# The order of the elements in the tile of exp(L): pairs of heads outermost or innermost

## The chip, the core and the metric

The kernel runs on one core of one Trainium2 chip. The metric is the device time of one execution in microseconds (us); lower is better. TensorE is called PE in the profile (its weight loads PEld), VectorE DVE, ScalarE ACT, GpSimd POOL, and SyncE, which issues most of the transfers, SP.

## What is computed

The reference is a gated recurrence over time, one state of 48 x 48 for each of 4 batches and 8 heads, and then a normalised two-layer perceptron with a residual:

```python
state = np.zeros((B, H, D, D), dtype=np.float32)          # B, H, S, D = 4, 8, 768, 48
for t in range(S):
    state = alpha[:, :, t, :, None] * state + np.einsum('bhd,bhe->bhde', k[:, :, t], v[:, :, t])
    y[:, :, t] = np.einsum('bhd,bhde->bhe', q[:, :, t], state)
x = y.transpose(0, 2, 1, 3).reshape(B, S, H * D)          # B, S, 384
xn = (x - mu) / np.sqrt(var + 1e-06) * g_ln
out = x + np.maximum(xn @ w_ch1, 0.0) @ w_ch2              # 384 -> 1536 -> 384
```

## The kernel before

Time is cut into 6 chunks of 128 steps. A chunk of one batch is one run of the generator `attention(c, b)`, so there are 24 of them; the kernel names them a, b, c, ... x in this order (a to d are chunk 0 for the four batches, e to h chunk 1, and so on). Within a chunk the recurrence becomes matrix products: with L the running sum of log(alpha), q is multiplied by exp(L) and k by exp(-L), and the state that goes into the next chunk is multiplied by a **gate**, which is exp(L) at the last step. Chunk 0 is treated as one piece of 128 steps, so it has one gate; each later chunk is treated as two halves of 64 steps and has two gates.

The partitions of a tile hold the 128 steps, and a row holds 8 heads x 48 channels. The heads are taken in pairs: a pair's two heads stand 64 apart, padded from 48 to 64, so that a transposed pair fills 112 partitions (R = 64 + 48). The steps of `attention` that matter here, with their lines:

- L289: log of alpha on ScalarE; L294 or L471: the running sums L on TensorE, into PSUM.
- L299: ScalarE writes exp(L) into the tile `eq`; L300: it writes exp(-L) back into PSUM. For the runs whose `eq` lies in a shared buffer, the profile calls that tile `more`.
- L302 and L304: VectorE multiplies k by exp(-L) and q by exp(L) into `qk`.
- L309: SP stores the rows of `eq` that hold the gates (one row in chunk 0, two after it) into a small buffer `row` in device memory, 2 KB a row.
- L320: TensorE transposes the pairs of `qk`; L325 and L327 copy the results out of PSUM (`kT`, `qT`). L337 and L487 are the scores, L346 and L351 mask them on VectorE.
- L357: SP fetches the gates from `row` as columns, one value for each of the 112 partitions and each of the 4 pairs, into the tile `gate`.
- L367: TensorE makes the update of the state. In chunk 0, L376 multiplies it by the gate on VectorE; in later chunks L380 adds on VectorE and L382 multiplies by the gate on GpSimd.
- L392 or L408: the output products; L417 to L460: the normalisation and a transpose into `xT`; L430 keeps x in device memory.

The weights arrive in twelve pieces as 64-bit numbers (L207). VectorE and ScalarE turn each into float32 (L219 to L229; VectorE reads and writes every second 32-bit word there). Three buffers hold the raw pieces, so a later piece is loaded only when an earlier one is decoded. The perceptron of chunk 0 is plain products (L514, L526); for later chunks the two layers are computed with fewer block products, whose operands VectorE prepares by sums (L586, L613, L752, L777), and whose results VectorE, ScalarE and GpSimd combine (L803 to L854 and L626 to L705).

All of these are generators. A string of letters and digits, `ORDER`, says which generator goes one step on next, and each engine runs its own instructions in that order. SP's queue is in that order too: a load that waits there holds back the loads behind it.

At the end of the kernel the tiles `eq` serve once more as plain buffers for sums of `xT` (L554 to L556), seen as flat rows.

Of the kernel before, what the change touches and what calls it, by code (L numbers as in the profile page):

```python
# [9 lines left out]
FP32 = mybir.dt.float32  # L10
# [38 lines left out]
def kernel(  # L49
# [36 lines left out]
    nc = tc.nc  # L86

    B, S, H, D = q.shape
    DM = H * D
    DF = w_ch1.shape[1]  # L90
    P = 128
    NCB = S // P
    NP = H // 2
    R = 64 + D
# [5 lines left out]
    cpool = ctx.enter_context(tc.tile_pool(name="const", bufs=1))  # L100
# [144 lines left out]
    for _ in range(8):  # L245
# [4 lines left out]


    shared = more.rearrange("p i m -> p (i m)")[:, :4 * NP * P]
    eqs = [cpool.tile([P, NP, 2, 64], FP32, name=f"eq{b}") for b in range(2)]
    eqs += [shared[:, i * NP * P:(i + 1) * NP * P].rearrange(
        "p (a b c) -> p a b c", b=2, c=64) for i in range(2)]
    qks = [cpool.tile([P, 2, NP, 2, 64], FP32, name=f"qk{b}") for b in range(3)]
    qks.append(shared[:, 2 * NP * P:].rearrange("p (i a b c) -> p i a b c", i=2, b=2, c=64))
    sts = [[cpool.tile([R, NP, D], FP32, name=f"st{b}_{i}") for i in range(2)] for b in range(B)]
    for b in range(B):
        nc.vector.memset(eqs[b].rearrange("p a b c -> p (a b) c")[:, :, D:], 0.0)  # L260
        nc.vector.memset(qks[b].rearrange("p i a b c -> p (i a b) c")[:, :, D:], 0.0)


# [1 line left out]
    def eq_of(c, b):  # L265
        return eqs[b if c < 2 else b % 2]

    def qk_of(c, b):
        return qks[b if c < 2 else b % 3]
# [10 lines left out]
    def attention(c, b):  # L280
# [3 lines left out]
        odd = 0 if whole else b % 2  # L284

        qk = qk_of(c, b).rearrange("t n p i c -> t n i p c")[:, :, :, :, :D]
        eq = eq_of(c, b).rearrange("t p i c -> t i p c")[:, :, :, :D]
        la = work.tile([P, 2, NP, D], FP32, name="la", tag="row", bufs=8)
        nc.scalar.activation(out=la, in_=raws.pop(("a", c, b)), func=AFT.Ln)  # L289
        las[c, b] = la.rearrange("t i p d -> t (i p d)")  # L290
# [14 lines left out]
        ends = slice(P - 1, P) if whole else slice(HS - 1, P, HS)  # L305
        ne = 1 if whole else 2
        row = dram.tile([2, 2 * 64 * NP], FP32, name="row", tag="row")
        gate = work.tile([P, 2, NP], FP32, name="gate", tag="gate", bufs=B)
        nc.sync.dma_start(row[:ne], eq_of(c, b)[ends].rearrange("o p i c -> o (p i c)"))  # L309
        yield  # L310
        at = ats[b % len(ats)]
        if not whole:
# [41 lines left out]
                mask=mask_of_halves.unsqueeze(1).broadcast_to([P, 2 * NP, HS]))  # L354
        yield
        with nc.allow_non_contiguous_dma(reason="two rows to columns"):
            nc.sync.dma_start(gate[:R, :ne], row[:ne].rearrange("o (p r) -> r o p", p=NP)[:R])  # L357
        yield
        vn = raws["v", c, b]
        heads = [slice(0, 64), slice(64, R)]  # L360
# [28 lines left out]
        for p in range(NP):  # L389
# [4 lines left out]
            for n in range(0 if whole else 8):  # L394

                if odd:
                    inner, s, i = n // 4, n // 2 % 2, n % 2
                    r = i
                else:
                    i, s, r = n // 4, n // 2 % 2, n % 2  # L400
# [144 lines left out]
    def buffers_of_last():  # L545

        more_x = work.tile([P, NF, B, P], FP32, name="xT", tag="xT").rearrange("p f b t -> p (f b t)")
        free = [raw.tile([P, 2, 2, NP, D], FP32, name=f"r{n}", tag="in", bufs=6).rearrange(
            "t b i p d -> t (b i p d)") for n in "akq"]
        h = [t.rearrange("k p i s t -> k (p i s t)") for t in ats]  # L550
        h += [t.rearrange("t n p i c -> t (n p i c)") for t in qks[:3]]
        h.append(more_x[:, :NT * HB * P])
        late_of["h"] = [t.rearrange("p (j b t) -> p j b t", b=HB, t=P) for t in h]
        sums = [t.rearrange("t p i c -> t (p i c)") for t in eqs[:2]]  # L554
        sums += [more_x[:, NT * HB * P:]] + [t[:, 512:] for t in free]
        late_of["x"] = [t[:, i * HB * P:(i + 1) * HB * P]  # L556
                        for t in sums for i in range(t.shape[1] // (HB * P))]
        late_of["u"] = [t[:, :512] for t in free]
# [198 lines left out]
    def combine_x(c):  # L757
        b = x_blocks(c)
        new = []
        if c + 1 == NCB:  # L760
            buffers_of_last()
            new = late_of["x"]
        for i in range(0 if new else 5):
            t = work.tile([P, NT, P], FP32, name=f"sum{i}", tag="sum", bufs=11)
            t = t.rearrange("p a t -> p (a t)")
            new += [t[:, k * HB * P:(k + 1) * HB * P] for k in range(2)]
        t101, t103, t100, m7, t102, m10, m9, m13, m8 = new[:9]
        add, sub = nc.vector.tensor_add, nc.vector.tensor_sub
        ready = x_ready(c)
        for n, op, out, x, y in (  # L770
                (None, sub, t101, b[1], b[3]), (2, sub, t100, b[4], b[5]),
                (1, add, t103, b[2], t100), (7, add, m7, t101, t103),
                (14, sub, t102, b[0], t100), (10, sub, m10, t102, t101),
                (3, sub, t101, t101, b[5]), (9, sub, m9, b[0], b[4]),
                (5, add, b[4], b[2], b[4]), (13, sub, m13, t103, b[3]),
                (8, sub, m8, t102, b[1])):
            op(out, x, y)  # L777
            if n is not None:
                ready[n] = out
            yield  # L780
# [99 lines left out]
    turns |= {"PQ"[h]: second_of_chunk_0(h) for h in range(2)}  # L880
    turns |= {"4": sums(), "5": scores()}
    turns |= {chr(ord("a") + n): attention(n // B, n % B) for n in range(NCB * B)}
    turns |= {chr(ord("A") + i): take_weights(i) for i in range(len(pieces))}
    turns |= {"M": mlp(), "V": hidden_products(NCB - 1), "S": combine_first(), "W": combine_weights(), "R": relus(),
# [34 lines left out]
```

## Time and profile before

| what | us |
|---|---|
| time, median of 3 runs | 432.96 (431.92 to 435.25) |
| the profiled execution's own time | 433.59 |
| its span in the profile | 431.5 |
| TensorE busy | 421.3 |
| VectorE busy | 331.7 |
| ScalarE busy | 205.8 |
| GpSimd busy | 151.8 |

The span is the time from the first to the last instruction of the program; busy time is the sum of an engine's instructions without overlap. The profile also has 52,797 packets of transfers, 45.36 MB in all. An instruction's line in a view reads: start, duration, engine, line of the kernel, operation, what it writes and reads, and in brackets how long its engine stood idle before it and what ended that. A group's line has the total busy time, the mean duration in ns, and the idle time before its members.

### The profile page before, as it was taken

What the parts mean: (1) busy time and instruction counts of PE and PEld (TensorE: products, weight loads), DVE (VectorE), ACT (ScalarE), POOL (GpSimd) and SP (SyncE); (2) the same over time, 40 slices, a digit from 0 to 9 for tenths busy, and PEclk for the clock granted to TensorE, in tenths of its full rate; (3) what the DMA queues carried; (4) which work ended last, traced back from release to release, by engine and by line L of the source; (5) the groups of instructions that cost most, each with busy time, mean ns of one, the idle gap of its engine ahead of it and who ended that gap; (6) DMA issues with size and microseconds to landing.
All of it is one profiled execution on the core that took longest, in us unless ns stands there. A gap on an engine that the chain in (4) does not pass through costs nothing.

```text
span 431.5 us, 11715 instructions
## 1 busy us (share of the span) xinstructions
PE 421.3 (98%) x4760; PEld 373.6 (87%) x4760; DVE 331.7 (77%) x634; ACT 205.8 (48%) x539; POOL 151.8 (35%) x171
## 2 busy tenths in 40 slices
PE   8998999999999999999999999999999999999995
PEld 6877888856788889998889988898998899999995
DVE  4997999899997978886758767657595669675972
ACT  6774566662763566714762443653527541311200
POOL 3020103010017381246561233671155652638323
PEclk9999999999999999999999999999999999999999
DMA  8878887896273343233413133301013000002101
GB/s 259 245 182 256 225 199 185 263 257 175 82 196 101 93 141 94 84 59 91 102 54 107 36 87 101 75 2 39 11 53 122 3 0 2 0 21 78 50 18 55
DMA packets 52797, 45.36 MB, mean 105 GB/s; under 512 B 24156, under 2 KB 48860, under 8 KB 52744
## 3 DMA queue, kind: packets, MB, share of 16 engines
q1 hardware_dynamic: 52344, 44.62, 37.3%
q8 instruction: 37, 0.61, 0.6%
q14 instruction: 16, 0.13, 0.1%
q10 hardware_dynamic: 400, 0.00, 0.1%
HBM read 35.08 MB, written 9.53 MB: 103 GB/s over the span
## 4 chain that ended last, share of the span: by engine, by line
PE 89%; DMA 6%; DVE 2%; issue 1%; SPq 1%; ACT 1%; DVEq 0%
PE ops L626 30%; PE hps L803 30%; PE ops L526 7%; PE hps L514 6%; PE yps L408 4%; DMA ws<-in_moe_w_ch_dram 3%; PE tps L320 3%; PE aps L487 2%; PE ups L367 2%; PE xps L453 2%; PE lps L471 1%; DMA vn<-in_v_dram 1%; DMA ra<-in_alpha_dram 1%; DMA gate<-row 1%; DVE w L221 0%
## 5 line engine op out<-in xcount | busy, mean ns | idle before, releaser
L642 POOL TENSOR_TENSOR ob<-ob,u 128x192 f32<-128x192 f32 x40 | 26.7, 678 | 69.2 <-DVE ob L639 53.2
L803 PE MATMUL hps<-sum,w 128*128 128x256 f32 x192 | 47.7, 380 | 0.0
L382 POOL TENSOR_TENSOR mid<-mid,gate 112x192 f32<-112x192 f32 x20 | 13.0, 652 | 90.4 <-DVE mid L380 40.5
L626 PE MATMUL ops<-w,hT 128*128 128x192 f32 x224 | 40.5, 327 | 0.0
L803 PEld LDWEIGHTS hps<-sum,w 128*128 128x128 f32 x192 | 35.8, 190 | 4.6
L626 PEld LDWEIGHTS ops<-w,hT 128*128 128x128 f32 x224 | 37.0, 190 | 0.5
L854 ACT ACTIVATE hT<-hT 128x512 f32<-128x512 f32 x48 | 28.2, 630 | 16.1 <-POOL hT L825 6.7
L803 PE MATMUL hps<-xT,w 128*128 128x256 f32 x136 | 35.1, 382 | 0.0
L514 PE MATMUL hps<-xT,w 128*128 128x256 f32 x144 | 33.0, 383 | 1.4 <-DVE w L229 1.4
L526 PE MATMUL ops<-w,hT 128*128 128x384 f32 x96 | 32.0, 488 | 0.0
L514 PEld LDWEIGHTS hps<-xT,w 128*128 128x128 f32 x144 | 26.6, 190 | 5.2 <-issue 1.5
L626 PE MATMUL ops<-ws,sum 128*128 128x192 f32 x160 | 28.6, 327 | 0.0
L803 PEld LDWEIGHTS hps<-xT,w 128*128 128x128 f32 x136 | 25.3, 190 | 3.3 <-DVE hT L835 0.2
L526 PEld LDWEIGHTS ops<-w,hT 128*128 128x128 f32 x96 | 17.8, 190 | 11.5 <-DVE w L229 0.3
L626 PEld LDWEIGHTS ops<-ws,sum 128*128 128x128 f32 x160 | 26.1, 190 | 0.1
L636 DVE TENSOR_TENSOR ob<-ops,ob 128x192 f32<-128x192 f32 x50 | 17.0, 352 | 11.2 <-PE ops L626 6.1
L626 PE MATMUL ops<-ws,hT 128*128 128x192 f32 x128 | 23.9, 328 | 0.9 <-issue 0.9
L327 ACT COPY qT<-tps 112x512 f32<-112x512 f32 x24 | 13.9, 585 | 22.8 <-PE tps L320 22.6
L320 PE MATMUL tps<-consts,qk 128*112 128x128 f32 x176 | 23.3, 273 | 0.4 <-DVE qk L304 0.4
L822 POOL TENSOR_TENSOR hT<-hT,u 128x512 f32<-128x512 f32 x8 | 10.9, 1357 | 33.8 <-DVE u L821 33.8
L320 PEld LDWEIGHTS tps<-consts,qk 128*112 128x112 f32 x176 | 20.0, 134 | 2.8 <-issue 1.1
L626 PEld LDWEIGHTS ops<-ws,hT 128*128 128x128 f32 x128 | 21.1, 190 | 1.4 <-issue 1.2
(240 smaller groups left out, 1130.5 us busy)
## 6 DMA issues: line engine op xcount, KB each, us to landing
ws<-in_moe_w_ch_dram SPq DMA_DIRECT2D x12, 768.0 KB
kept<-x SPq DMA_DIRECT2D x24, 192.0 KB
ob<-kept SPq DMA_DIRECT2D x24, 192.0 KB
vn<-in_v_dram SPq DMA_DIRECT2D x20, 192.0 KB
rq<-in_q_dram SPq DMA_DIRECT2D x18, 192.0 KB
rk<-in_k_dram SPq DMA_DIRECT2D x18, 192.0 KB
ra<-in_alpha_dram SPq DMA_DIRECT2D x16, 192.0 KB
out_dram<-ob SPq DMA_DIRECT2D x14, 192.0 KB
```

The costliest lines, as they stand in the source:

```text
L320: nc.tensor.transpose(tps[:, p], qk_of(c, b)[:, i, p].rearrange("p a b -> p (a b)")[:, :R], ident)
L327: nc.scalar.copy(out=qT, in_=tv)
L382: nc.gpsimd.tensor_mul(new, new, by)
L408: nc.tensor.matmul(yps[r][halves[s], i, p], of, by, start=not (odd and inner), stop=bool(inner or not odd), skip_group_check=bool(odd))
L514: nc.tensor.matmul(hps, w1[:, j // 2, f, j % 2 * P:][:, :P], xT_of[0][:, f, bs], start=(f == 0), stop=(f == NF - 1))
L526: nc.tensor.matmul(ops_of[b], hT_of[c][:, j, b], w2[:, j], start=(j == 0), stop=(j == NJ - 1))
L626: nc.tensor.matmul(acc, lhs[:, j], rhs[:, j], start=(j == 0), stop=(j == NT - 1))
L636: nc.vector.tensor_add(x, acc, x)
L642: getattr(nc.gpsimd, f"tensor_{op}")(x, x, y)
L803: nc.tensor.matmul(acc[:, i], w, b, start=True, stop=True)
L822: add_late(c4, c4, u2)
L854: nc.scalar.activation(out=x, in_=x, func=AFT.Relu)
```

## The change

The tile `eq` had the order (pair, head of the pair, channel): each head's 48 channels were neighbours. It now has the order (head of the pair, channel, pair): the four pairs' values for one channel are neighbours, and neighbouring channels of one head are four values (16 bytes) apart. The row that is stored for the gates is the same 2 KB in the new order, so that the four values that one partition of `gate` needs stand side by side in it: the fetch has pieces of 16 bytes where it had pieces of 4. ScalarE's exponential (L299) writes `eq`, and VectorE's product with q (L304) reads it, through views that walk the tile in the old order of elements.

```diff
-    eqs = [cpool.tile([P, NP, 2, 64], FP32, name=f"eq{b}") for b in range(2)]
+    eqs = [cpool.tile([P, 2, 64, NP], FP32, name=f"eq{b}") for b in range(2)]
     eqs += [shared[:, i * NP * P:(i + 1) * NP * P].rearrange(
-        "p (a b c) -> p a b c", b=2, c=64) for i in range(2)]
+        "p (a b c) -> p a b c", a=2, b=64) for i in range(2)]
...
-        nc.vector.memset(eqs[b].rearrange("p a b c -> p (a b) c")[:, :, D:], 0.0)
+        nc.vector.memset(eqs[b][:, :, D:], 0.0)
...
-        eq = eq_of(c, b).rearrange("t p i c -> t i p c")[:, :, :, :D]
+        eq = eq_of(c, b).rearrange("t i c p -> t i p c")[:, :, :, :D]
...
-        nc.sync.dma_start(row[:ne], eq_of(c, b)[ends].rearrange("o p i c -> o (p i c)"))
+        nc.sync.dma_start(row[:ne], eq_of(c, b)[ends].rearrange("o i c p -> o (i c p)"))
...
-            nc.sync.dma_start(gate[:R, :ne], row[:ne].rearrange("o (p r) -> r o p", p=NP)[:R])
+            nc.sync.dma_start(gate[:R, :ne], row[:ne].rearrange("o (r p) -> r o p", p=NP)[:R])
...
-        sums = [t.rearrange("t p i c -> t (p i c)") for t in eqs[:2]]
+        sums = [t.rearrange("t i c p -> t (i c p)") for t in eqs[:2]]
```

## The prediction

> **What bounds the kernel now.** I read the busy table first, then busy time by stage, then the chain that ended last in its first 45 us, then VectorE in order of time, then the costs of the lines touched.
>
> ```profile
> PE 421.3 (98%) x4760; PEld 373.6 (87%) x4760; DVE 331.7 (77%) x634; ACT 205.8 (48%) x539; POOL 151.8 (35%) x171
> ```
>
> TensorE is busy for 98% of the span; from 42.29 us to 427.18 us the chain shows it idle twice, for 0.84 and 0.92 us. So the time is settled by when TensorE's stream starts, by any holes torn into it, and by a short end. By stage (us, then busy us of PE, PEld, DVE, ACT, POOL, the granted clock, the DMA share and GB/s):
>
> ```profile
> 7.40:42.20 34.80, 32.31 (x631) 27.50 (x629) 30.55 (x55) 24.06 (x64) 2.77 (x3) 1.00 0.86 247
> 62.00:83.00 21.00, 20.98 (x479) 18.22 (x475) 19.12 (x38) 15.21 (x36) 4.16 (x5) 1.00 0.72 186
> 83.00:131.00 48.00, 48.00 (x519) 33.07 (x512) 45.62 (x81) 25.55 (x67) 4.74 (x9) 1.00 0.67 189
> ```
>
> VectorE (DVE) is 88% busy before the stream starts and 91 and 95% in the two later stages; after 131 us it has room (215.5 us busy of 301). The chain at the start:
>
> ```profile
> 12.87 2.23 DMA gate<-row
> ...
> 15.30 0.36 DVE st L376
> 15.66 0.26 SPq L139
> ...
> 16.48 7.57 DMA ws<-in_moe_w_ch_dram
> ...
> 30.13 6.61 DMA ws<-in_moe_w_ch_dram
> ...
> 36.76 0.57 DVE w L219
> ```
>
> A load queued on SP (L139) waits for the multiply by the gate (L376) on VectorE. The first piece of weights is issued behind it, VectorE decodes that piece, the second piece follows, and its decoding ends at 42.14, when TensorE's stream begins. A gate's fetch is on this chain, but see what stands before L376 on VectorE (start, duration, idle before it in brackets):
>
> ```profile
> 9.70 0.69 DVE L325 COPY kT<-tps 112x512 f32<-112x512 f32 x1 [0.31 <-PE tps L320]
> 14.07 1.35 DVE L346 COPY_PREDICATED at<-consts,aps 128x512 f32<-128x512 int32 x2
> 15.30 0.67 DVE L376 TENSOR_TENSOR st<-ups,gate 112x192 f32<-112x192 f32 x2
> 22.11 0.48 DVE L443 TENSOR_SCALAR xn<-x,few 128x384 f32<-128x384 f32 x1 [1.13 <-ACT few L440]
> 24.07 0.56 DVE L219 TENSOR_SCALAR w<-ws 128x768 int32<-128x768 int32 x1 [0.21 <-DMA ws<-in_moe_w_ch_dram]
> 36.76 0.56 DVE L219 TENSOR_SCALAR w<-ws 128x768 int32<-128x768 int32 x1 [1.19 <-DMA ws<-in_moe_w_ch_dram]
> ```
>
> The second L346 ends at 15.42, so L376 would not have started earlier had its gate landed earlier.
>
> **The change, part by part.** No instruction is added, removed or moved; the two memsets have the same size. What changes is the packets of the gate's fetch (L357), and that the exponential (L299) writes, and the product with q (L304) reads, the tile in steps of 16 bytes, where both ran over 48 neighbours.
>
> ```profile
> DMA packets 1475, 0.02 MB, mean 8 GB/s; under 512 B 1465, under 2 KB 1473, under 8 KB 1475
> q1 hardware_dynamic: 1475, 0.02, 41.5%
> gate<-row SPq DMA_DIRECT2D x20, 3.5 KB
> ```
>
> *The gate's packets.* The first two lines are the DMA view of 64 to 66 us, which holds little but gates: 41.5% of 2 us of 16 engines for 1475 packets, 9 ns each. A gate of 3.5 KB in 4-byte pieces is 896 packets, 0.50 us of all 16 engines; in 16-byte pieces it is 224. I price those at the same 9 ns: a record moving 768 bytes takes 36 ns, so 16 bytes are near the 4-byte end. That frees 0.38 us a gate (0.19 for the four half-sized ones of chunk 0), some 8.3 us of DMA time in all. On the path it buys little. L376 gains nothing, as shown. The first weights can gain at most the 0.21 us that VectorE waited for them. The second weights are issued at 30.13, behind the two half-sized gates issued at 22.11 and 22.55: at most 2 x 0.5 us if all queued transfers close up, and VectorE's own work ends only 1.19 us before they land. After 42 us a gate is awaited by GpSimd (34.0 us in all, 5 times), and VectorE waits for GpSimd there only once for 0.30 us. Bounds 0 and -1.2 us; I take -0.2, as the DMA share is 0.86 and the queue isn't full.
>
> *The 16-byte steps.* No row has such a step. The nearest have 8 bytes:
>
> ```profile
> L299 ACT ACTIVATE eq<-lps 128x384 f32<-128x384 f32 x20 | 9.8, 491 | 10.4 <-PE lps L471 9.3 <-issue 1.1
> L304 DVE TENSOR_TENSOR qk<-rq,eq 128x384 f32<-128x384 f32 x20 | 11.2, 562 | 0.0
> L227 DVE SCALAR_TENSOR_TENSOR ws<-ws 128x768 int32<-128x768 int32 x12 | 11.5, 960 | 1.1 <-ACT ws L225 1.0
> L586 DVE TENSOR_TENSOR more<-ws,w 128x768 f32<-128x768 f32 x3 | 2.8, 952 | 0.0
> ```
>
> L227 reads and writes every second word and takes 960 ns, against 952 for neighbours: 8 bytes cost nothing. So the low end is 0. The high end is that L227 already covered its 6144 bytes of tile as fast as VectorE can: 384 elements at 16 bytes cover the same 6144 and would take 960 ns, 0.40 more than L304's 562, which is also twice the 1.05 ns per element between sizes of this line's kind. On ScalarE, L225 covers 6144 bytes in 1025 ns, which bounds L299 at +0.53; twice the slope between L417 (192 elements, 329 ns) and L421 (384, 487 ns) gives +0.32. I take +0.40 and +0.32, the ends of halved speed, because no VectorE row with two inputs covers its tile faster than L227 does.
>
> [...]
>
> *Where that lands.* **Before 42 us:** the first exponential delays the first product by 0.32; the products of a, b, c, d stand ahead of L376 with no idle time but the 0.31 at 9.70: 0.32 + 4 x 0.40 - 0.31 = 1.6 us later, and with it L139 and the first weights. The products e and f (0.80) fit under the 1.13 and 0.21 us of idle at 22 and 24 us, g and h (0.80) under the 1.19 at 36.76: nothing more if that cover holds, up to 1.6 if not. **62 to 83 us:** TensorE's transposes (L320) start behind the products with a slack of 0.71 (i), 0.22 (j), 3.08 (k) and 0.31 us (l). j comes 0.80 late: a hole of 0.6. By l VectorE is 1.6 behind less the idle 0.56 before L219 at 75.59, of which half is real, so 1.3 against 0.6 + 0.31: another 0.4. **83 to 131 us:** m has 10.1 and n 1.34 us of slack; VectorE then waits for TensorE itself (0.42 at L530), so only o's 0.40, right ahead of the sums (L777) that L803 needs, can come through; I take half, 0.2. **Later** slacks are 3.9 us and up: nothing.
>
> Sum: 1.6 + 0.6 + 0.4 + 0.2 - 0.2 = +2.6 us. The profiled execution took 433.59 (span 431.5, 2.1 around it): 436.2. The median of the three runs is 432.96, 0.6 lower, so several runs may come out near 435.6. A difference of under 1% (4.3 us) is about what a measurement of this kernel can tell from no change.
>
> **The rivals.** *The steps cost nothing.* For it: the 8-byte rows, and L219, which reads every second word of 768 in 557 ns, half the time per element, so VectorE can cover ground twice as fast as in L227. Against: L219 has one input and another pace than L304's. Then only the gates count: 0 to -1.2 us, 432.4 to 433.6. This is the other side: not slower. It decides if L304 stays near 0.56 us. [...]
>
> *VectorE becomes the bound up to 131 us.* Its idle time is mostly waits for weights (0.56, 0.74) whose loads wait for buffers that VectorE frees, so those waits move with it and cover nothing. Then the fifteen products a to o come through: 15 x 0.40 + 0.32 = 6.3 us, 439.9. For it: 95% busy. Against: TensorE has no hole in that stage, so it runs behind VectorE by an unseen slack. It is over 1% once 4.4 of the 6.3 come through.
>
> *The first 42 us are bound by the small packets.* If the gate's 2.23 us on the chain, both waits for weights (0.21, 1.19) and a queue closing up by 0.8 all went, 4.4 us would be saved: 429.2. Against: VectorE is 88% busy there and L346 covers the gate.
>
> *The change does not do what it says*: 16-byte pieces still sent as 4-byte packets. The sum then moves by 0.2, so it is no case of its own.
>
> **How the numbers follow.** Forecast 0.38, with its own 434.5 to 438.5; of this 0.10 lies over 437.3, past 1%. VectorE as the bound 0.34. Free steps 0.22. Small packets 0.06. Slower by over 1%: 0.10 + 0.34 = 0.44; within 1%: 0.28 + 0.22 = 0.50; faster by over 1%: 0.06. The range runs from free steps seen from the median (433.0 - 1.2 = 431.8) to 6.3 us and a little of the ScalarE bound above the profiled run, 440.5.
>
> **What would show it.** Right: L304 near 960 ns and L299 near 806; some 38,000 packets instead of 52,797; the first weights issued near 18.1 instead of 16.48; L514's stream beginning near 43.9; a hole ahead of the transposes at about 67 us. Wrong: L304 unchanged, or the stream beginning late by much less than 1.6 us though L304 is slow.

## The result and the profile after

| | before | after |
|---|---|---|
| time, median (range; runs) | 433.99 us (431.92 to 436.39; 21) | 435.99 us (434.51 to 438.51; 21) |
| ratio to before | | 1.0048, 95% interval 1.0032 to 1.0064 |
| profiled execution: own time, span | 433.59, 431.5 | 437.41, 435.3 |

The change costs 0.48%, some 2.1 us (1.4 to 2.8). That is under the 1% named in the prediction, but its interval excludes no change. The profiled execution of after lies 1.4 us over its own median, so its trace can't be subtracted from that of before line by line; below it is read together with the other traces.

The first part of the profile after is its total of packets, where before had 52,797, and the groups of the lines that the change touches (busy us, mean ns; idle before):

```profile
DMA packets 38013, 45.36 MB, mean 104 GB/s; under 512 B 9372, under 2 KB 34076, under 8 KB 37960
```

```profile
L320 PE MATMUL tps<-consts,qk 128*112 128x128 f32 x176 | 23.9, 274 | 2.3 <-DVE qk L304 2.2
...
L299 ACT ACTIVATE eq<-lps 128x384 f32<-128x384 f32 x20 | 17.6, 879 | 10.2 <-PE lps L471 9.4 <-ACT lps L300 0.8
L304 DVE TENSOR_TENSOR qk<-rq,eq 128x384 f32<-128x384 f32 x20 | 17.4, 872 | 0.0
L300 ACT ACTIVATE lps<-lps 128x384 f32<-128x384 f32 x24 | 14.6, 606 | 0.0
```

The fetch did change, by 14,784 packets. The two strided instructions became slow: L304 by 0.31 us (562 to 872 ns), L299 by 0.39 (491 to 879). L300, which the change doesn't touch, became slow too (494 to 606 ns). TensorE's transposes (L320) waited 2.2 us for L304 where they had waited 0.4; all but 0.4 us of that lies before the stream.

By stage, with the columns of before (us, then busy us of PE, PEld, DVE, ACT, POOL, the granted clock, DMA share, GB/s):

```profile
7.40:42.20 34.80, 30.33 (x502) 25.38 (x501) 30.76 (x52) 26.07 (x64) 2.75 (x3) 1.00 0.76 235
62.00:83.00 21.00, 20.51 (x382) 16.96 (x381) 20.39 (x37) 15.20 (x34) 3.78 (x5) 1.00 0.60 157
83.00:131.00 48.00, 47.79 (x641) 32.51 (x640) 44.82 (x79) 29.62 (x74) 4.52 (x8) 1.00 0.65 197
```

From 62 to 83 us VectorE is busy 20.39 of 21.00 us (19.12 before), and TensorE, which had 0.02 us free there, has 0.49. From 83 to 131 us TensorE still has next to no idle time. The chain that ended last, at the start (start, us, what):

```profile
13.24 1.34 DVE at L346 x2
...
14.93 0.71 DVE more L304
...
15.71 1.36 DVE at L346 x2
17.07 0.06 SPq L139
...
17.69 9.12 DMA ws<-in_moe_w_ch_dram
26.84 0.57 DVE w L219
```

The gate's fetch is off this chain; slow products stand on it. L139 is released at 17.07 where it was 15.66, and the first weights are issued at 17.69 where it was 16.48. Their transfer then took 9.12 us instead of 7.57. This looks like an accident of this execution: the kernel with 16-byte steps and 4-byte fetches (experiment 2) issued them at 17.69 too and decoded them at 25.18, not 26.84, and with 16-byte fetches in experiment 6 the same transfer took 7.48. TensorE's stream (L514) begins at 45.02, before at 42.29. In both it waits for the decoding (L229), with less idle time ahead of it after than before:

```profile
42.29 9.31 PE L514 MATMUL hps<-xT,w 128*128 128x256 f32 x42 [1.41 <-DVE w L229]
...
45.02 9.31 PE L514 MATMUL hps<-xT,w 128*128 128x256 f32 x42 [0.19 <-DVE w L229]
```

### The profile page after: what moved, and what is told of

It is laid out like the page before. It is cut to its first block, busy times and chain, and to the rows that moved or that the text cites. A ratio compares the mean times of both kernels' runs of the same rounds, so it can differ in the third digit from the quotient of the medians.

```text
span 435.3 us, 11715 instructions
## 1 busy us (share of the span) xinstructions
PE 422.2 (97%) x4760; PEld 373.0 (86%) x4760; DVE 338.3 (78%) x634; ACT 214.8 (49%) x539; POOL 153.7 (35%) x171
## 2 busy tenths in 40 slices
DMA packets 38013, 45.36 MB, mean 104 GB/s; under 512 B 9372, under 2 KB 34076, under 8 KB 37960
## 4 chain that ended last, share of the span: by engine, by line
PE 81%; DVE 9%; DMA 5%; ACT 2%; issue 1%; SPq 1%; DVEq 0%; ACTq 0%
PE ops L626 30%; PE hps L803 30%; PE ops L526 7%; PE yps L408 3%; PE tps L320 3%; DMA ws<-in_moe_w_ch_dram 3%; PE aps L487 2%; PE ups L367 2%; PE xps L453 2%; DVE w L221 2%; DVE ws L227 1%; DVE w L229 1%; PE lps L471 1%; DVE qk L304 1%; DMA rq<-in_q_dram 1%
## 5 line engine op out<-in xcount | busy, mean ns | idle before, releaser
L514 PE MATMUL hps<-xT,w 128*128 128x256 f32 x144 | 33.0, 383 | 0.2 <-DVE w L229 0.2
L514 PEld LDWEIGHTS hps<-xT,w 128*128 128x128 f32 x144 | 26.6, 190 | 4.0 <-issue 0.3
L320 PE MATMUL tps<-consts,qk 128*112 128x128 f32 x176 | 23.9, 274 | 2.3 <-DVE qk L304 2.2
L320 PEld LDWEIGHTS tps<-consts,qk 128*112 128x112 f32 x176 | 19.9, 134 | 5.7 <-issue 1.8
L299 ACT ACTIVATE eq<-lps 128x384 f32<-128x384 f32 x20 | 17.6, 879 | 10.2 <-PE lps L471 9.4
```

The costliest lines, as they stand in the source:

```text
L299: nc.scalar.activation(out=eq, in_=lv, func=AFT.Exp)
L320: nc.tensor.transpose(tps[:, p], qk_of(c, b)[:, i, p].rearrange("p a b -> p (a b)")[:, :R], ident)
L514: nc.tensor.matmul(hps, w1[:, j // 2, f, j % 2 * P:][:, :P], xT_of[0][:, f, bs], start=(f == 0), stop=(f == NF - 1))
```

## The experiments

All ratios are to the kernel before, run on the same chip beside it. They are worked out over all the runs and need not be the quotient of the two medians. A difference of two ratios has the intervals of both, added as squares; 0.001 is 0.43 us. In all but the seventh and the eighth, gates or exponentials reach the products in another order, so the values are not those of the reference; the eighth computes none of them.

**1. The larger packets alone.** The kernel before, with its tile in the old order, fetches the gates in 16-byte pieces.

```diff
-            nc.sync.dma_start(gate[:R, :ne], row[:ne].rearrange("o (p r) -> r o p", p=NP)[:R])
+            nc.sync.dma_start(gate[:R, :ne], row[:ne].rearrange("o (r p) -> r o p", p=NP)[:R])
```

> The kernel before with one edit: the gate's fetch takes pieces of 16 bytes from the row as it is stored (so the gates' values are out of order); the exponential and the product keep their old steps. It measures the packets alone. My theory (the loss is the 16-byte steps on VectorE and ScalarE, the packets free little): 0 to -1.0 us against the kernel before, the stream of L514 starting 0 to 1 us earlier than 42.3, 38,013 packets. Rival (the packets free much, and the steps cost that much more than is seen): -1.5 us or more.

> The first experiment once more (the kernel before, the gates fetched in pieces of 16 bytes, so that the gates' values come in another order), on another chip: its ratio of 0.999 (0.9963 to 1.0016) left open whether the larger packets bring anything. Theory A, the packets are worth 1.1 us where no product is slow: 0.9975, some 432.9 where the kernel before has 434.0. Theory B, the prediction's 0.2 us: 0.9995. An interval that holds both leaves it open.

Measured: 432.73 us against 433.30, ratio 0.999 (0.9963 to 1.0016), and on the other chip 434.04 against 434.23, 0.9993 (0.9964 to 1.0022). Together 0.9991, give or take 0.0020: -0.4 us, from -1.3 to +0.5. A gain of 1 us is still inside, no gain is as well, and 4.4 us is excluded. L299 and L304 stayed at 490 and 562 ns, with 38,013 packets. The two traces differ. On the first chip the stream begins at 39.60 us, earlier than the 0 to 1 us that I had expected, and VectorE waits for neither piece of weights (its L219 at 22.75 and at 34.27 have no idle time before them); four of the twelve runs there took 430.65 to 430.71 us, under every run of before on that chip. On the second chip the stream begins at 42.39, and no run is below 431.63. So the smaller number of packets may now and then take the weights off the path; the intervals don't show it.

**2. The 16-byte steps alone.** The kernel after, with the 4-byte fetch.

```diff
-            nc.sync.dma_start(gate[:R, :ne], row[:ne].rearrange("o (r p) -> r o p", p=NP)[:R])
+            nc.sync.dma_start(gate[:R, :ne], row[:ne].rearrange("o (p r) -> r o p", p=NP)[:R])
```

> The changed kernel with one edit back: the gate is fetched in pieces of 4 bytes again (so its values are out of order); the tile keeps its new order. It measures the 16-byte steps alone. My theory: +2 to +3 us against the kernel before, that is the changed kernel plus 0 to 1.0 us; L304 near 870 ns, L299 near 880 ns. Rival (the packets free much): 1.5 us or more above the changed kernel.

Measured: 435.42 us against 433.30, ratio 1.005 (1.0027 to 1.0073), with 52,797 packets, L304 at 870 ns and L299 at 877. The steps alone give the whole loss of after (1.0048), to within 1.2 us.

**3 and 4. Only the write, only the read.** In the first kernel L299 writes in steps and L304 reads 48 neighbours; in the second it is the other way round. Both have the 16-byte fetch.

```diff
+        flat = eq_of(c, b).rearrange("t i c p -> t (i c p)").rearrange(
+            "t (p i c) -> t i p c", i=2, c=64)[:, :, :, :D]
# only the write (another place):
-        nc.vector.tensor_mul(qk[:, 0], raws.pop(("q", c, b)), eq)
+        nc.vector.tensor_mul(qk[:, 0], raws.pop(("q", c, b)), flat)
# only the read (another place):
-        nc.scalar.activation(out=eq, in_=lv, func=AFT.Exp)
+        nc.scalar.activation(out=flat, in_=lv, func=AFT.Exp)
```

> The changed kernel, except that the product with q reads the tile as 48 neighbours (other values): only ScalarE's write has 16-byte steps. Theory that VectorE, 88 to 95% busy, carries most of the loss: L299 stays near 880 ns, L304 back at 560 ns, and the time is within 0.8 us of the kernel before. Rival (ScalarE's later exponentials delay the first products and the running sums, and carry the loss): at least 1.3 us above the kernel before.

> The changed kernel, except that the exponential writes the tile as 48 neighbours (other values): only VectorE's read has 16-byte steps. Theory that VectorE carries most of the loss: L304 near 870 ns, L299 back at 490 ns, +1.3 to +2 us against the kernel before. Rival (ScalarE carries it): within 0.7 us of the kernel before. If both this and the write-only kernel are near the kernel before, the two delays add on one path and neither is enough alone.

Measured: write 433.46 us, 1.0004 (0.9984 to 1.0024); read 433.62 us, 1.0008 (0.9990 to 1.0026). The groups of lines of the first (L299 to L304 are L301 to L306 there):

```profile
L301 ACT ACTIVATE eq<-lps 128x384 f32<-128x384 f32 x20 | 17.6, 879 | 10.1 <-PE lps L473 9.3 <-ACT lps L302 0.8
...
L302 ACT ACTIVATE lps<-lps 128x384 f32<-128x384 f32 x24 | 14.6, 606 | 0.0
...
L306 DVE TENSOR_TENSOR qk<-rq,eq 128x384 f32<-128x384 f32 x20 | 11.2, 561 | 0.0
```

and of the second, with a line of its TensorE in order of time:

```profile
L306 DVE TENSOR_TENSOR qk<-rq,eq 128x384 f32<-128x384 f32 x20 | 17.4, 872 | 0.0
...
L302 ACT ACTIVATE lps<-lps 128x384 f32<-128x384 f32 x24 | 11.8, 492 | 0.0
...
L301 ACT ACTIVATE eq<-lps 128x384 f32<-128x384 f32 x20 | 9.8, 491 | 11.0 <-PE lps L473 9.4 <-issue 1.1 <-PE lps L296 0.6
```

```profile
65.72 1.49 PE L322 MATMUL tps<-consts,qk 128*112 128x128 f32 x12 [0.39 <-DVE qk L306]
```

Each instruction is slow by itself. The second exponential (606 ns) is slow only behind a first one that writes in steps. The hole ahead of the transposes comes with the slow read and not with the slow write. In time, neither kernel is clear of the kernel before: that the read alone would cost 1.3 to 2 us was wrong (0.3, give or take 0.8). Against experiment 1 (0.9991) the write costs 0.6 us and the read 0.7, each give or take 1.2; after stands 2.5 above experiment 1 (give or take 1.1). Whether the two add up or are worse together can't be told from these.

**5 and 6. Where the steps cost.** Steps only in the runs a to d (chunk 0), and only in i to x (chunks 2 to 5); the 16-byte fetch everywhere. In these two, in experiment 4 and in the next one the kernel also clears the whole of the tiles `eq` at its start and not their padding alone; VectorE stands idle for 3.1 us or more after that, ahead of its first product, so this costs nothing.

```diff
+        eq = eq if c == 0 else flat      # the first; the second: c >= 2
```

> The changed kernel with the 16-byte steps in chunk 0 alone (runs a to d, the products ahead of L376); all later runs write and read the tile as 48 neighbours (their gates' values are out of order). My theory: this is the part before the stream, so L376 starts near 16.95 us as in the changed kernel, the stream of L514 starts 0.5 to 1.5 us late, no hole ahead of the transposes near 67 us, and +0.7 to +1.5 us against the kernel before. Rival (the delay ahead of L376 is swallowed by the transfers, and the loss comes from the runs after it): within 0.4 us of the kernel before.

> The changed kernel with the 16-byte steps from chunk 2 on (runs i to x); runs a to h write and read the tile as 48 neighbours (their gates' values are out of order). My theory: L376 back near 15.3 us, the stream on time, a hole of about 0.4 us ahead of j's transposes and one or two of 0.1 to 0.2 near l, and +0.4 to +1.1 us against the kernel before. Rival of the run before: +1.5 us or more, with more holes in the stream.

Measured: a to d 434.96 us against 434.22, 1.0008 (0.9984 to 1.0032); i to x 435.61 us, 1.0034 (1.0011 to 1.0056). Against experiment 1: 0.7 us for a to d (give or take 1.4), 1.9 for i to x (give or take 1.3). Together they make 2.6, the 2.5 of after, so nothing is left for e to h (give or take 1.8).

Against the kernel before, both came out otherwise than I had expected: a to d cost 0.3 us and not 0.7 to 1.5, with L376 at 16.41 and the stream at 42.52, only 0.2 late; i to x cost 1.5 us and not 0.4 to 1.1, with the holes that were expected (0.39 ahead of j's transposes, 0.14 at 82.2) but the stream at 43.15, 0.9 late although no product ahead of it is slow. The intervals of both reach into the expected ranges, so the times decide neither.

**7. The runs e to h.** The order of after and its 16-byte fetch in chunk 1 alone; all the other runs walk the tile and fetch the gates as before.

```diff
+        steps = c == 1
+        eq = eq_of(c, b)
+        if not steps:
+            eq = eq.rearrange("t i c p -> t (i c p)").rearrange("t (p i c) -> t i c p", i=2, c=64)
...
+ ... row[:ne].rearrange("o (r p) -> r o p" if steps else "o (p r) -> r o p", p=NP)[:R])
```

> The 16-byte steps and the 16-byte fetch in the runs e to h only (chunk 1); all the other runs keep the old order of the tile and pieces of 4 bytes, all values right. Theory A: the four slow products of e to h stand under VectorE's waits for weights and cost nothing, and the fetches of e to h shorten the wait for the second weights: 0.998 to 0.999, 0.4 to 0.9 us below the kernel before. Theory B, VectorE has no cover there: 4 x 0.30 less 0.2, 1.0 us above the kernel before (1.0023).

Measured: 433.51 us against 434.23, ratio 0.9982 (0.9959 to 1.0006). A full price for four slow products (1.0023) is excluded. Its VectorE in order of time (L304 is L308 there; idle before in brackets):

```profile
19.04 0.85 DVE L308 TENSOR_TENSOR qk<-rq,eq 128x384 f32<-128x384 f32 x1
20.19 0.86 DVE L308 TENSOR_TENSOR qk<-rq,eq 128x384 f32<-128x384 f32 x1
...
33.14 0.86 DVE L308 TENSOR_TENSOR qk<-rq,more 128x384 f32<-128x384 f32 x1 [0.89 <-DMA rq<-in_q_dram]
34.30 0.87 DVE L308 TENSOR_TENSOR more<-rq,more 128x384 f32<-128x384 f32 x1
36.78 0.56 DVE L219 TENSOR_SCALAR w<-ws 128x768 int32<-128x768 int32 x1 [0.68 <-DMA ws<-in_moe_w_ch_dram]
```

All four products are slow, and the second weights are decoded at 36.78, as before (36.76): VectorE's wait ahead of them is 0.68 instead of 1.19. The slow products of g and h went into that wait. The stream begins at 42.29, to the hundredth where it did. This version is at the kernel before or slightly under it; the interval holds no difference, so it isn't shown to be faster. The last section has what the granted clock adds to this.

**8. The price of a step by itself.** A kernel without the rest: products on VectorE that read one input, or write the result, in steps of 4 to 32 bytes, and exponentials on ScalarE that write or read in such steps, four of each; then fetches of a gate in both kinds of pieces.

In outline (on the chip the reading and writing products alternate):

```python
for s in (1, 2, 3, 4, 6, 8):                      # step in elements of 4 bytes
    nc.vector.tensor_mul(res, a, steps(src))      # L41, four times
    nc.vector.tensor_mul(steps(dst), a, a)        # L43
    nc.scalar.activation(out=steps(exp), in_=lps, func=AFT.Exp)   # L45
    nc.scalar.activation(out=cop, in_=steps(src), func=AFT.Exp)   # L47
```

> None of the work of the reference: a ladder of single operations of 128x384 with inner steps of 4, 8, 12, 16, 24 and 32 bytes, four each: VectorE's product reading such a step (tiles res<-plain,rd) and writing it (dw<-plain), ScalarE's exponential writing it (aw<-lps) and reading it (cop<-rd); then a gate's fetch in pieces of 4 and of 16 bytes on an idle queue, each followed by a copy that waits for it. If the price is per 16 bytes touched: 4 and 8 bytes free, 12 bytes about half the price of 16, 16 to 32 bytes the same, near 870 ns (VectorE) and 880 ns (ScalarE). If it grows with the ground covered: 8 bytes free, 16 bytes near 870, 32 bytes near 1500 ns. If only reads or only writes pay, the other stays near 560 or 490 ns. The fetch: 0.3 to 1.0 us shorter with 16 bytes.

VectorE in order of time, one reading product for steps of 4, 12, 16 and 32 bytes:

```profile
4.52 0.55 DVE L41 TENSOR_TENSOR res<-plain,rd 128x384 f32<-128x384 f32 x1
...
11.08 0.67 DVE L41 TENSOR_TENSOR res<-plain,rd 128x384 f32<-128x384 f32 x1
...
17.79 0.84 DVE L41 TENSOR_TENSOR res<-plain,rd 128x384 f32<-128x384 f32 x1
...
34.62 0.85 DVE L41 TENSOR_TENSOR res<-plain,rd 128x384 f32<-128x384 f32 x1
```

Mean ns of the four instructions of 128x384 by step (the first reading product, 495 ns, is left out):

| step in bytes | 4 | 8 | 12 | 16 | 24 | 32 |
|---|---|---|---|---|---|---|
| VectorE, reading | 551 | 552 | 670 | 853 | 845 | 855 |
| VectorE, writing | 550 | 553 | 680 | 850 | 848 | 860 |
| ScalarE, writing | 491 | 540 | 734 | 869 | 872 | 890 |

An 8-byte step is free on VectorE (552 ns for 551), 12 bytes lie between (670), and from 16 to 32 bytes the price stays the same (845 to 855). So it isn't the ground covered that counts. An estimate fits the numbers: with the 1.05 ns per element of the prediction (in before L586 takes 952 ns for 768 elements and L302 547 for 384), 148 of the 551 ns are fixed; the rest is 1.36 ns per element at 12 bytes and 1.84 at 16. Counted in pieces of 16 bytes, at 12 bytes three elements in four begin a new one, at 16 bytes and over each does: 1.36/0.75 and 1.84/1 are both 1.8 ns per new piece. At 8 bytes that would be 0.9 ns, less than the 1.05 of the element itself, and no price was measured there. The fetches of the ladder landed 2.1 us (4 bytes) and 1.9 us (16 bytes) after their issue, but told little, as both kinds were under way at the same time; the 0.3 to 1.0 us that I had expected was not seen. The transfers' own records do tell it: in before a packet of 4 bytes took 9.0 ns on average, and in after the 4,928 packets of 16 bytes took 8.6.

## Why the prediction was right in its sum, and where its terms were off

*Forecast: +2.6 us, 436.2. Measured: +2.1 (1.4 to 2.8), 435.99.* That 436.2 and 435.99 lie so close is luck in part: the base, 433.59, was 0.4 under the median of 21 runs, and the sum 0.5 over what was measured.

**The price of a step.** L304 was put at 960 ns and came at 872; L299 at 806 and came at 879. The choice of the slow end was right. The bound behind it was wrong in kind: it took L227 as the fastest that VectorE covers ground, and the ladder shows no ground counted, since 32 bytes cost what 16 do (855 and 853 ns). The error was 0.09 us a product. That L300 becomes slow too (+0.11 us, 24 times) was not in the sum. The records of neighbours on ScalarE overlap, so the two prices don't add in full: from start to start L299 takes 0.65 us where it took 0.37 and L300 0.52 where it took 0.41, together 0.39 more. ScalarE, 49% busy, is taken to have had room for it.

**Before the stream: 1.6 us.** With the measured prices the same sum is 0.39 + 4 x 0.31 - 0.31 = 1.3 us. Single traces scatter by as much as 0.8 us here: L376 starts at 15.30, 15.38, 16.12, 15.64 and 16.02 in the five traces without steps in a to d (before, experiment 1 twice, 6, 7), mean 15.7, and at 16.95, 17.03 and 16.41 in the three with steps in both lines (after, 2, 5), mean 16.8. So VectorE is 1.1 us late there, give or take 0.6. That the single trace of after showed 1.65 is closer to the forecast than it deserves. The stream's own start scatters more: 42.29, 39.60, 42.39, 43.15 and 42.29 in the five, and 45.02, 43.59 and 42.52 in the three. In the last of these, experiment 5, it is late by 0.2 us, which the prediction had named as a sign that it is wrong; one trace can't decide that. What experiment 5 measures in whole time is 0.7 us, give or take 1.4: the term looks too big, but 1.6 is not excluded.

**e to h: nothing, if VectorE's waits cover them.** Shown by experiment 7 to within 0.3 us (the gain of its own larger packets, and what the last section says of the clock, are in that number), and the cover can be seen shrinking from 1.19 to 0.68.

**62 us and later: 0.6 + 0.4 + 0.2 = 1.2 us.** The hole ahead of the transposes of j is there. TensorE of after, in order of time:

```profile
67.83 0.49 PE L320 MATMUL tps<-consts,qk 128*112 128x128 f32 x3
68.70 1.49 PE L320 MATMUL tps<-consts,qk 128*112 128x128 f32 x12 [0.38 <-DVE qk L304]
```

It is 0.38 long, 0.39 in experiments 4 and 6 and 0.38 in experiment 2, and missing from before and from experiments 1, 3, 5 and 7, that is wherever L304 isn't slow in i and j. Two products at 0.31 less the slack of 0.22 are 0.40: slack and place were read rightly, only the price of a product was too high. Of l's 0.4 nothing is seen that waits for VectorE: in after a hole of 0.11 ahead of its transposes (82.5) and one of 0.21 ahead of the scores at 86.1 both end with a ScalarE instruction (L517 and L299), and experiment 2 has neither. The sum had no such term. o's 0.2 is not seen.

The holes make 0.70 us together, while experiment 6 gives 1.9 us for i to x, give or take 1.3. The traces speak for the holes: each engine's instructions have one order, so the time from the stream's start to the end of the span compares the same work, and it is 389.7 to 390.7 us in the four traces with slow reads in i to x (after, 2, 4, 6) against 389.0 to 389.6 in before, experiment 1 on its first chip, 3 and 7 (the other two traces hold the stretch of slow clock of the last section). That is some 0.8 us, and the term of 1.2 was too big by 0.4. A loss later on is not seen: from 135 to 425 us TensorE is busy for 288.6 us in after and 288.3 in before. Of the 2.1 us this leaves 1.3 before the stream, which is what the measured prices give there; that is an estimate from single traces.

**The packets: -0.2 us.** Measured -0.4 (-1.3 to +0.5) where the products are fast, and nothing visible between experiment 2 and after, where they are slow (give or take 1.2). The 8.3 us of DMA time that the fetches should free was right: the packets of 4 and 16 bytes take 13.6 us of all 16 engines in before and 5.3 in after. Nearly all of it is off the path, as the profile said: L346 stood ahead of L376. One reading was loose and nothing hangs on it: the 34.0 us in five waits of GpSimd for a gate are of the whole span; after 42 us it is four waits, 23.5 us.

**The rivals.** *Free steps* falls with L304 at 872 ns. *VectorE as the bound* would be 0.39 + 15 x 0.31 = 5.0 us at the measured prices; the measured 2.1 (at most 2.8) excludes it, and experiment 7 shows why, since four of its products cost nothing: the waits for weights did serve as cover. *Bound by small packets* falls with experiment 1. *The change doesn't do what it says* falls with the 38,013 packets.

## What to carry to other kernels

Before a layout is turned to suit a transfer, look at who else walks the tile: here each gate's fetch lost three quarters of its packets off the path, and 48 instructions on VectorE and ScalarE paid for it. A slower instruction costs only where the slack behind it is smaller than its price, so read the idle time ahead of its consumer, run by run: e to h had it (1.19 us ahead of the second weights, of which 0.68 was left), j lacked 0.4 us. Where a turned layout is wanted all the same, turn it in the runs whose engines wait anyway; here that lost nothing that could be measured (experiment 7: 0.9982, 0.9959 to 1.0006).

## What the runs showed of the hardware

**Price by step.** On VectorE reads and writes pay alike: 8-byte steps are free (552 and 553 ns for 551 and 550), 12-byte steps take 670 and 680 ns, and 16-byte steps 853 and 850, about what 32-byte ones take (855 and 860). ScalarE shows a small loss at 8 bytes already (491 to 540 ns). By the estimate of experiment 8 VectorE pays some 1.8 ns per new piece of 16 bytes against 1.05 ns per element. That pieces of 16 bytes are what counts is the author's reading of these prices; no run shows the cause.

**A strided write slows the next exponential.** L300 reads and writes PSUM as before, and takes 606 ns behind a strided exponential and 492 behind a plain one (experiments 3 and 4). It is not only its record that is longer: the next instruction starts 0.52 us after it in after, where it is 0.41 in before.

**The granted clock halves for 3.4 us in two of the traces.** The trace of experiment 1 on its second chip, by stage and for the stretch inside:

```profile
42.20:62.00 19.80, 19.61 (x141) 16.83 (x142) 17.62 (x26) 9.48 (x23) 1.48 (x3) 0.91 0.83 223
...
43.10:46.50 3.40, 3.40 (x10) 2.67 (x9) 3.17 (x6) 1.27 (x2) 0.97 (x2) 0.51 0.89 275
```

The clock is 0.51 from 43.10 to 46.50 us and 1.00 on both sides, and the 42 products (L514) that start at 42.39 take 10.99 us where they take 9.31 in before. Experiment 5's trace, with a mean clock of 0.995, has the same stretch. These are the two traces in which TensorE stood idle longest right ahead of its stream, for 1.61 and 1.71 us; the others have at most 1.56.

Over all runs this goes with the change. Such a stretch takes 0.004 off the mean clock of a run of 432 us, and of the traces here only these two have a mean of 0.996 or less. So low a mean stands in 13 of the 76 runs of before in the experiments, which took 1.5 to 2.2 us longer on average than the others of their chip, and in 16 of the 60 runs of experiments 1, 3, 5 and 6. It stands in none of the 52 runs of after and of experiments 2, 4 and 7, that is of the kernels with slow reads in e to h. In the traces of these four TensorE stands idle for 0.19 to 0.88 us ahead of its stream; in three of them (after, 2 and 7) part of the idle time stands ahead of the transposes of g and h instead. So the slow products of e to h seem to spare the kernel this stretch now and then, which would be worth 0.3 us on average (13 of 76 times some 1.9 us), and may be why experiment 7 came out under the kernel before. That the idle time brings the slow clock is not shown: no run varied it alone, and in the traces of experiments 1 (first chip) and 6 it is as short, 0 and 0.44 us, though other runs of theirs have the low clock.

Single runs of one kernel here lie up to 6 us apart (431.63 to 437.57 in experiment 1 on its second chip); such stretches may be part of that. With these numbers of runs the intervals stay near 1 us, and a term of 0.5 us can't be measured through the whole kernel's time.
